# Gated multi-query attention with a SiLU layer: other planner constants, weight pieces split in one go, and O's upper half cast by a transfer

## The chip, the cores and the metric

The kernel runs on one core of one Trainium2 chip. The metric is the device time of one execution in microseconds, the median of several runs. Beside the timed runs there is one profiled execution of the kernel before; "the page" is the summary of its trace, and the other views named below are answers drawn from the same trace.

## The reference

For 2048 rows x of width 512 the kernel computes two branches and mixes them row by row with a gate:

```python
q = (x @ wq).reshape(B, S, 32, 16).transpose(0, 2, 1, 3)     # 32 heads of 16
k, v = x @ wk, x @ wv                                         # one key and value head for all
p = softmax(einsum("bhqd,bkd->bhqk", q, k) * 16 ** -0.5)
a = einsum("bhqk,bkd->bhqd", p, v).transpose(0, 2, 1, 3).reshape(B, S, 512) @ wo
b = silu(x @ w1) @ w2                                         # 512 -> 1792 -> 512
g = sigmoid((x * gate_w).sum(-1, keepdims=True))
out = g * a + (1 - g) * b
```

All in float32: x is (1, 2048, 512), w1 (512, 1792), w2 (1792, 512). The kernel keeps float32 accuracy on a 16-bit matrix engine by writing each operand as an upper and a lower float16 part and adding three products (upper by upper, upper by lower, lower by upper).

## The kernel before, in words

**Tiling.** The rows are in four chunks c of 512, the 32 heads in four groups o of eight. A *round* is one (c, o); there are 16. In a round the 2048 keys are walked in 32 *steps* of 64 keys. A step has two halves j, each with one 128x1024 tile of scores: `scores` (L1224, eight matmuls of 50x32 weights into the PSUM tile `S`, of which there are two), then `exponential` (L1230, ACT, from `S` into half of a probability buffer `P`). So there are 1024 score tiles and 1024 exponentials. There are four buffers `P`, and as the chunks of the input `xs` are used up for good, each of the first three becomes another (`XUSE = "PPP "`).

**P times V.** A finished step is multiplied with V in one of two ways. *Whole* (W): eight float32 matmuls with `VF`, in one go or as two halves N and M of 256 columns each. *Split* (A and B): VectorE (DVE) first computes the lower part of the two halves with two subtractions (`low`, L1236, 128x1024 each, into a tile `L`, a spent weight buffer `raw`, or, in the change, a spent chunk of `xs`); then TensorE takes eight matmuls of the upper bfloat16 half of `P` (A) and eight of the lower part (B). A buffer `P` is free again when W or M has run, or when A and both subtractions have.

**The rest.** The feed-forward layer, the q projections and the output projection are matmuls into `pm` (L848), 64 rows of two different products at a time; a group of eight such matmuls is called a pass F here. An output of the first layer goes through a tanh on ACT (L909), a multiply on DVE (L912), a cast of the upper part by a transfer that GpSimd's queue issues (L921) and a subtraction for the lower (L925).

**What sets the order.** The program is written out once, at build time, by a small planner inside `attention`. It keeps a clock for TensorE (PE), ScalarE (ACT) and DVE with fixed costs (`PASS`, `EXP`, `LOW`, ...) and lets the engine that is free first take its next job; the result is a fixed instruction order for each engine, and on the chip only semaphores wait. For PE the choice is in `pe_next`: scores first (priority 0), then P V that is urgent (1), the feed-forward passes while they are behind their quota (2), other P V (3 or 4), and feed-forward beyond the quota (5). P V is urgent in `pv_next` when

```python
p = 1 if n_exp[0] - 2 * s >= 2 * n_bufs[0] + LAG - 8 or ... else 3 if ab else 4
```

that is, when the exponentials have run so many halves ahead of step s that its buffer is about to be needed. A job that can't be interrupted is taken only if it ends before the next score tile is due, with `SLACK` to spare. DVE's jobs are entries `task(due, ready, length, f)`.

**Weights.** `Pieces` (L159 and on) brings w1, wq, w2 and wo in 36 pieces through two buffers `raw`; `step` (L200) writes the upper part of a new piece (L207) and the lower part of the piece before (L208), and asks GpSimd's queue for the next piece (L190). `piece_next` (L1387) spaces the steps by `PACE`.

**Shifts and the fallback test.** Each of the 15 later q blocks gets a bound that is subtracted from its scores (`q_shift`, L433): 8 rows of 512 numbers go to DRAM (`sh`), and DVE takes their minimum (L440) for a test. The minima, and largest values of inputs and weights, are collected by `chores` one by one on DVE; the flag at the end decides whether a slow second pass runs. With these inputs it doesn't.

**End of a round.** `finish` runs four DVE jobs `norm_a`, `norm_x`, `norm_y`, `norm_b` (transposes and the division), and `norm_c` then splits the result into `O`, upper and lower half (L134, L135), for the output projection of the chunk. The last round does this in two halves (`finish_half`).

## Time and profile before

| what | value |
|---|---|
| median of 3 timed runs | 1021.53 us (1020.79 to 1023.5) |
| the profiled execution's own time | 1022.62 us |
| its span, first to last instruction | 1020.8 us |
| busy: PE, ACT, DVE, POOL | 998.8, 987.1, 913.9, 59.4 us |
| granted TensorE clock | 0.999 |

The profiled execution is 1.09 us above the median of the runs, and its span 1.8 us below its own time. Matmuls and activations overlap the next one of their kind in the trace, so a busy share near 100% doesn't say that an engine runs at its rate: what counts is the distance from start to start. A row of the timeline gives the start, the length of a merged stretch, the engine, the line, what is written from what, and how many instructions are merged; in brackets the idle time before it and what ended that.

### The profile page before, as it was taken

To read this page: it belongs to the slowest core of one execution; us is meant where nothing else is said; L and a number is where in the kernel's file an instruction comes from. 1 tells how busy PE (TensorE), PEld (TensorE's weight loads), DVE (VectorE), ACT (ScalarE), POOL (GpSimd) and SP (SyncE) were. 2 spreads that over 40 slices of the span, in tenths; PEclk is the share of its full clock that TensorE was granted. 3 is DMA by queue.
4 is the path that set the end of the run, shared out by engine and by line. 5 is a ranking of instruction groups with operands and counts; after the bars stand their busy time and mean duration, and the time that the engine had idled before them with its cause. 6 is when DMAs were issued, how large, how long until landed. Compare 5 with 4: busy or idle time off the path is not lost.

```text
span 1020.8 us, 67262 instructions
## 1 busy us (share of the span) xinstructions
PE 998.8 (98%) x31528; PEld 590.4 (58%) x31528; DVE 913.9 (90%) x1177; ACT 987.1 (97%) x1108; POOL 59.4 (6%) x138
## 2 busy tenths in 40 slices
PE   8999999999999999999999999999999999999996
PEld 6455555555555556556565655656565555656754
DVE  7888888889999999999999899999988989889983
ACT  5999999999999999999999999999999999999994
POOL 4111111100000000000000000000000000000000
PEclk9999999999999999999999999999999999999999
DMA  5132321211101111101101111001201110011001
GB/s 210 50 96 77 82 55 53 69 40 41 25 10 45 30 36 20 29 11 35 31 4 42 40 41 25 26 14 26 50 11 25 36 46 15 19 21 25 4 4 47
DMA packets 28105, 39.98 MB, mean 39 GB/s; under 512 B 5689, under 2 KB 19370, under 8 KB 27818
## 3 DMA queue, kind: packets, MB, share of 16 engines
q0 software_dynamic: 10656, 15.73, 7.4%
q1 hardware_dynamic: 16442, 19.27, 5.9%
q8 instruction: 248, 4.06, 1.6%
q10 hardware_dynamic: 720, 0.59, 0.2%
q14 instruction: 39, 0.32, 0.1%
HBM read 19.98 MB, written 8.25 MB: 28 GB/s over the span
## 4 chain that ended last, share of the span: by engine, by line
PE 48%; issue 24%; ACT 17%; DVE 6%; DMA 3%; POOL 1%; SPq 0%; ACTq 0%; POOLq 0%; DVEq 0%
PE pm L848 19%; PE pv L1261 15%; ACT P L1230 12%; PE S L1224 12%; ACT xs L1230 4%; DVE L L1236 2%; DMA raw<-in_B_w_dram 1%; ACT e L909 1%; DVE raw L1236 1%; DMA H<-e 1%; POOL raw L190 1%; DVE e L912 1%; PE pv L1249 1%; DMA xn<-in_A_x_dram 1%; POOL H L921 0%
## 5 line engine op out<-in xcount | busy, mean ns | idle before, releaser
L1230 ACT ACTIVATE P<-S 128x1024 f32<-128x1024 f32 x776 | 741.2, 1094 | 9.3 <-PE pv L1261 3.7
L1224 PE MATMUL S<-qb,KT 50*32 50x512 f16 x8096 | 447.2, 379 | 7.5 <-ACT P L1230 3.5
L1224 PEld LDWEIGHTS <-KT 50*32 50x32 f16 x8096 | 203.2, 89 | 226.3 <-issue 134.0
L1236 DVE TENSOR_TENSOR L<-P 128x1024 f16<-128x1024 f32 x248 | 296.6, 1219 | 28.9 <-ACT P L1230 25.2
L848 PE MATMUL pm<-xs,w1s 64*32 64x512 f16 x5376 | 258.0, 375 | 0.9 <-DVE e L912 0.9
L1230 ACT ACTIVATE xs<-S 128x1024 f32<-128x1024 f32 x248 | 246.7, 1097 | 0.7 <-PE S L1224 0.3
L848 PE MATMUL pm<-w2s,H 64*32 64x512 f16 x5376 | 240.0, 375 | 0.8 <-DVE e L912 0.3
L1261 PE MATMUL pv<-P,VF 64*32 64x512 f32 (+1 forms) x3888 | 225.4, 510 | 0.1
L1236 DVE TENSOR_TENSOR raw<-P 128x1024 f16<-128x1024 f32 x126 | 151.4, 1219 | 6.4 <-ACT P L1230 6.1
L848 PEld LDWEIGHTS <-w1s 64*32 64x32 f16 x5376 | 116.8, 93 | 45.3 <-issue 6.0
L848 PEld LDWEIGHTS <-H 64*32 64x32 f16 x5376 | 112.7, 93 | 43.4 <-issue 4.8
L848 PE MATMUL pm<-xs,wqs 64*32 64x512 f16 x1440 | 101.3, 375 | 0.2
L1236 DVE TENSOR_TENSOR L<-xs 128x1024 f16<-128x1024 f32 x78 | 93.5, 1218 | 4.9 <-ACT xs L1230 4.6
L1261 PEld LDWEIGHTS <-VP 64*32 64x32 f16 x4000 | 75.2, 93 | 34.8 <-issue 4.3
L1261 PEld LDWEIGHTS pv<-P,VF 64*32 64x32 f32 x3888 | 79.6, 106 | 20.6 <-issue 2.4
L1261 PE MATMUL pv<-L,VP 64*32 64x512 f16 x1304 | 88.4, 375 | 0.1
L1261 PE MATMUL pv<-P,VP 64*32 64x512 bf16 x1496 | 83.3, 387 | 0.0
L921 POOL DMA_DIRECT2D H<-e x56 | 29.7, 530 | 709.2 <-DVE e L912 661.9
L848 PE MATMUL pm<-wo_s,O 64*32 64x512 f16 x1440 | 66.3, 375 | 0.1
L1261 PE MATMUL pv<-xs,VF 64*32 64x512 f32 (+1 forms) x1072 | 64.4, 531 | 0.0
L1236 DVE TENSOR_TENSOR raw<-xs 128x1024 f16<-128x1024 f32 x48 | 57.9, 1217 | 4.7 <-ACT P L1230 2.1
L1261 PE MATMUL pv<-raw,VP 64*32 64x512 f16 x696 | 55.2, 375 | 0.0
(215 smaller groups left out, 668.0 us busy)
## 6 DMA issues: line engine op xcount, KB each, us to landing
H<-e POOLq DMA_DIRECT2D x56, 128.0 KB, 2.5
raw<-in_B_w_dram POOLq DMA_DIRECT2D x24, 256.0 KB, 3.2
qb<-qd SPq DMA_DIRECT2D x180, 32.0 KB
xn<-in_A_x_dram SPq DMA_DIRECT2D x8, 512.0 KB
out_dram<-acc SPq DMA_DIRECT2D x14, 256.0 KB
qd<-qx SPq DMA_DIRECT2D x13, 256.0 KB
raw<-in_A_wo_dram POOLq DMA_DIRECT2D x4, 256.0 KB, 3.2
qb<-sh SPq DMA_DIRECT2D x60, 2.0 KB
```

Source lines behind the costliest of these rows:

```text
L190: queue.dma_start(r, src)
L848: nc.tensor.matmul(self.bank[32 * m:32 * m + 32], l(i, rows, 32 * m), r(j, rows), start=first, stop=last)
L909: nc.scalar.activation(e, o.bank, AF.Tanh, scale=t_scale)
L912: nc.vector.scalar_tensor_tensor(e, e, 1.0, o.bank, op0=OP.add, op1=OP.mult)
L921: nc.gpsimd.dma_start(H[:, 0], e)
L1224: nc.tensor.matmul(sc[32 * m:32 * m + 32, f], KT[b:b + 50, k0:k0 + 32], qtile[i][b:b + 50, m // 2, j], start=True, stop=True)
L1230: nc.scalar.activation(probs[s][:, 2 * j:2 * j + 2], banks.pop(p), AF.Exp, scale=scale_of(*rounds[steps[s][0]]))
L1236: nc.vector.tensor_tensor(lows[s, j], probs[s][:, js], upper(probs[s])[:, js], op=OP.subtract)
L1249: nc.tensor.matmul(pvs[i][h][32 * j:32 * j + 32, 256 * q:256 * q + 256], VF[r, NK - 2 * PAIRS + 2 * u + a], probs[s][r, j, 256 * a:256 * a ...
L1261: nc.tensor.matmul(pvs[i][h][32 * j:32 * j + 32, q], a[r], b[r, q], start=k == 0 and n != "B", stop=k == NK - 1 and n in "BMW")
```

## The change

It edits constants of the planner and four pieces of code:

1. `SLACK` 0.1 to 0.05, `LAG` 7 to 6, `GAP` 0.3 to 0.2, and the term `BOW`, which let the feed-forward fall behind its quota by up to 40 passes in mid-program, goes. A step's P V so becomes urgent one exponential sooner.
2. `XUSE`: the third chunk of `xs` becomes four tiles for lower parts instead of a seventh buffer `P`.
3. `Pieces.step` writes both parts of a piece one behind the other, and `piece_next` gives steps later due times.
4. `norm_c` asks GpSimd's queue for a casting transfer for O's upper half; a new DVE job `norm_d` subtracts, planned 3.0 us later.
5. The 15 minima on DVE go; instead 15 transfers on SyncE's queue (`shift_rows`) bring the first halves of the shifts back from DRAM into `wqs` when the last q block is done, and one reduction finds the least.

```diff
-LOAD, SLACK, ROOM, LAG, QUOTA, HB, EB, LB, PACE, START, WAIT, HOLD = 3.5, 0.1, 3.6, 7, 1.7, 7, 2, 3, 5.6, 0.3, 0.2, 0.4
+LOAD, SLACK, ROOM, LAG, QUOTA, HB, EB, LB, PACE, START, WAIT, HOLD = 3.5, 0.05, 3.6, 6, 1.7, 7, 2, 3, 5.6, 0.3, 0.2, 0.4
-BOW = 40 / 2.0 ** 18
-HALVES, GAP = True, 0.3
+HALVES, GAP = True, 0.2
-XUSE = "PPP "
+XUSE = "PPL "
...
         def step(self, by_scalar=False):
-            new = self.raws.pop(0) if self.raws else None
-            if new:
-                r, a1, a2, scale, what = new
-                if by_scalar:
-                    nc.scalar.activation(a1, r, AF.Copy, scale=scale)
-                else:
-                    nc.vector.tensor_scalar(a1, r, scale, None, op0=OP.mult)
-                self.rest.append((what, lambda: nc.vector.scalar_tensor_tensor(a2, r, scale, a1, op0=OP.mult, op1=OP.subtract)))
-            if len(self.rest) > bool(new):
+            while self.rest and (len(self.rest) > 1 or not by_scalar):
                 what, second = self.rest.pop(0)
                 second()
                 self.done.append(what)
                 self.load(nc.gpsimd)
+            if self.raws:
+                r, a1, a2, scale, what = self.raws.pop(0)
+                second = lambda: nc.vector.scalar_tensor_tensor(a2, r, scale, a1, op0=OP.mult, op1=OP.subtract)
+                if by_scalar:
+                    nc.scalar.activation(a1, r, AF.Copy, scale=scale)
+                    self.rest.append((what, second))
+                else:
+                    nc.vector.tensor_scalar(a1, r, scale, None, op0=OP.mult)
+                    second()
+                    self.done.append(what)
+                    self.load(nc.gpsimd)
...
-        return lambda: nc.vector.tensor_reduce(um[:, n:n + 1], s1, axis=AX.X, op=OP.min)
...
+        def shift_rows():
+            for n in range(1, NO * NCH):
+                nc.sync.dma_start(wqs[8 * n - 8:8 * n, 0, 0], sh[n % NO, n // NO][:, 0])
...
-            nc.vector.tensor_reduce(mr[0:64], um, axis=AX.X, op=OP.min)
+            nc.vector.tensor_reduce(mr[0:rows_], wqs[0:rows_, 0, 0], axis=AX.X, op=OP.min)
+            nc.vector.tensor_tensor(mr[0:64], mr[0:64], um, op=OP.min)
...
+                elif XUSE[c] == "L":
+                    l_free.extend((t, flat_x[:, 1024 * n:1024 * n + 1024].rearrange("p (a n) -> p a n", a=2)) for n in range(4))
...
             O = wp.tile([128, 2, 512], F16, name="O", bufs=NO)
-            split_v(O[:, 0], O[:, 1], st["OT"])
+            nc.gpsimd.dma_start(O[:, 0], st["OT"])
+            task(t + CAST + 4, t + CAST, 0.62, lambda t: norm_d(st, key, O, t))
+
+        def norm_d(st, key, O, t):
+            nc.vector.tensor_tensor(O[:, 1], st["OT"], O[:, 0], op=OP.subtract)
...
-                task((n - 4.6) * PACE, max((n - 6) * PACE, t + LOAD if n > 1 else 0.0), 1.3, run)
+                task((n + 1) * PACE, max((n - 1) * PACE, loaded[-2] if len(loaded) > 1 else 0.0), 1.2, run)
...
-                    cands.append((r, 4.5 if near else 2 if work.passes < QUOTA * p + 3 * KD * len(early) - 30 - BOW * p * (2 * len(steps) - p) else 5, "F", None))
+                    cands.append((r, 4.5 if near else 2 if work.passes < QUOTA * p + 3 * KD * len(early) - 30 else 5, "F", None))
```

Because the planner decides anew from the first edit on, the whole order of PE differs. Counted over the first pass, 261 of the 512 steps are split instead of 250, 79 are whole in two halves instead of 54, and 166 whole in one go instead of 202; six steps at the end have a form of their own in both.

**A buffer near the start.** The rows are PE's and ACT's, with buffer numbers. Exponentials are counted from 0; number 34, whose input is `S_1476` before and `S_1497` in the change, writes into `P_576`, which an earlier step still holds. PE before, around the P V of that earlier step:

```order
L1224 LDWEIGHTS KT_60
L1224 MATMUL S_1509<-qb0_83,KT_60 32x512
L1261 MATMUL pv0_791<-P_576,VF_63 32x512
L1261 MATMUL pv1_792<-P_576,VF_63 32x512
L848 LDWEIGHTS wqs_73
```

and the same P V in the change (here the second half of columns, M; N stands one score tile earlier):

```order
L1233 LDWEIGHTS KT_60
L1233 MATMUL S_1385<-qb0_83,KT_60 32x512
L1270 MATMUL pv0_792<-P_576,VF_63 32x256
L1270 MATMUL pv1_793<-P_576,VF_63 32x256
L851 LDWEIGHTS wqs_73
```

ACT before, and then in the change, where these score tiles are used:

```order
L1230 ACTIVATE P_578<-S_1369 128x1024
L1230 ACTIVATE P_575<-S_1392 128x1024
L1230 ACTIVATE P_575<-S_1434 128x1024
L1230 ACTIVATE P_576<-S_1476 128x1024
L1230 ACTIVATE P_576<-S_1509 128x1024
```

```order
L1239 ACTIVATE P_578<-S_1385 128x1024
L1239 ACTIVATE P_575<-S_1424 128x1024
L1239 ACTIVATE P_575<-S_1458 128x1024
L1239 ACTIVATE P_576<-S_1497 128x1024
L1239 ACTIVATE P_576<-S_1537 128x1024
```

Before, the P V that empties `P_576` stands behind both score tiles that are to go into it; in the change it stands ahead of the two tiles before those.

**The end.** DVE's rows from the last transpose of the first half of the last round on. Before:

```order
L1174 STREAM_TRANSPOSE O<-U 128x256
L1150 STREAM_TRANSPOSE T_33427<-pv_31790 128x256
L1150 STREAM_TRANSPOSE T_33427<-pv_31791 128x256
L1154 TENSOR_TENSOR T_33427<-T_33427 128x16x15
L1157 TENSOR_TENSOR U<-T_33427,nus 128x112
```

In the change:

```order
L1179 STREAM_TRANSPOSE O<-U 128x256
L830 SCALAR_TENSOR_TENSOR acc<-pm,gg,acc 128x512
L1155 STREAM_TRANSPOSE T_33593<-pv_31955 128x256
L1155 STREAM_TRANSPOSE T_33593<-pv_31956 128x256
L830 SCALAR_TENSOR_TENSOR acc<-pm,gg,acc 128x512
L1159 TENSOR_TENSOR T_33593<-T_33593 128x16x15
L1162 TENSOR_TENSOR U<-T_33593,nus 128x112
```

Two sums of the output projection (`acc<-pm,gg,acc`) have moved into the last normalisation; on PE the last 4.5 passes of that projection now stand behind the last P V, where before no such pass was left.

More of the change, by code (lines that the diff above doesn't have):

```diff
@@ L109 @@
     kab = consts.tile([128, 32], F16)
-    um = consts.tile([64, NO * NCH], F32)
+    um = consts.tile([64, 1], F32)
     qx = consts.tile([128, 1024], F16)
@@ L131, in split @@
         nc.vector.scalar_tensor_tensor(a2, a, scale, a1, op0=OP.mult, op1=OP.subtract)
-    def split_v(a1, a2, a):
-        nc.vector.tensor_copy(a1, a)
-        nc.vector.tensor_tensor(a2, a, a1, op=OP.subtract)
     def product3(p, lhs, rhs, first, last):
@@ L438, in q_shift @@
             nc.sync.dma_start(sh[o, c][4 * h:4 * h + 4, 0], s1[32 * h:32 * h + 4])
-        n = c * NO + o
-        return lambda: nc.vector.tensor_reduce(um[:, n:n + 1], s1, axis=AX.X, op=OP.min)
     def first_pass(pO):
@@ L722, in chores @@
         todo.append(lambda: absmax(mxs[:, M_VV:M_VV + 1], VF[:, :, 1:17], AX.XY))
+        rows_ = 8 * (NO * NCH - 1)
+        def shift_rows():
+            for n in range(1, NO * NCH):
+                nc.sync.dma_start(wqs[8 * n - 8:8 * n, 0, 0], sh[n % NO, n // NO][:, 0])
         def gather():
             mt, mr, mq = sc[:, 0:32], sc[:, 32:33], sc[:, 64:96]
-            nc.vector.tensor_reduce(mr[0:64], um, axis=AX.X, op=OP.min)
-            nc.vector.tensor_scalar(mxs[0:64, M_B:M_B + 1], mr[0:64], -1.0, SHIFT * LAM / ONE, op0=OP.mult, op1=OP.add)
+            nc.vector.tensor_reduce(mr[0:rows_], wqs[0:rows_, 0, 0], axis=AX.X, op=OP.min)
+            nc.vector.tensor_tensor(mr[0:64], mr[0:64], um, op=OP.min)
+            nc.vector.tensor_scalar(mxs[0:rows_, M_B:M_B + 1], mr[0:rows_], -1.0, SHIFT * LAM / ONE, op0=OP.mult, op1=OP.add)
             nc.vector.transpose(mt, mxs)
@@ L753, in verdict @@
             nc.vector.tensor_copy(flag, g[:, 0, 0:1])
-        return todo, gather, row, *(lambda n=n: check(n) for n in range(0, len(RANGES), 3)), verdict
+        return todo, shift_rows, gather, row, *(lambda n=n: check(n) for n in range(0, len(RANGES), 3)), verdict
     def row_maxima(g0, gs, gp, wqs, qsc):
@@ L884, in x_used @@
                     n_bufs[0] += 1
+                elif XUSE[c] == "L":
+                    l_free.extend((t, flat_x[:, 1024 * n:1024 * n + 1024].rearrange("p (a n) -> p a n", a=2)) for n in range(4))
+                    l_free.sort(key=lambda x: x[0])
                 elif XUSE[c] == "H":
@@ L1037, in shift @@
                 new.wait = t
-                note = q_shift(o, c, s1)
+                q_shift(o, c, s1)
                 shifted.add((o, c))
                 def close(t):
-                    note()
                     open_q.pop()
@@ L1047, in close @@
                         e_left[0] += 1
-                task(t + 9, t, 0.6, close)
+                task(t + 4, t + 2, 0.02, close)
             task(t, t, 0.6, shift, True)
@@ L1385, in pack_next @@
                 task(t + 4, t, length, run)
+        loaded = []
         def piece_next(t):
@@ L1391, in run @@
                     split_pieces.step()
+                    loaded.append(t + LOAD)
                     piece_next(t)
                 n = split_pieces.count
-                task((n - 4.6) * PACE, max((n - 6) * PACE, t + LOAD if n > 1 else 0.0), 1.3, run)
+                task((n + 1) * PACE, max((n - 1) * PACE, loaded[-2] if len(loaded) > 1 else 0.0), 1.2, run)
             else:
@@ L1405, in chore_next @@
             elif len(chores) > 1:
-                task(t + 16, lambda: None if open_q else t, 1.1, lambda t: (chores.pop(1)(), chore_next(t)))
+                task(t + 16, lambda: None if open_q else t + 4, 1.1, lambda t: (chores.pop(1)(), chore_next(t)))
         def finish(i, t):
@@ L1426, in fourth @@
                 norm_b(state)
-                task(t + 6, lambda: t if projected[0] >= NO * c else None, 1.15, lambda t: norm_c(state, (c, o), t))
+                task(t + 6, lambda: t if projected[0] >= NO * c else None, 0.02, lambda t: norm_c(state, (c, o), t))
             task(t, lambda: t if idle[0] else None, 1.25, first)
```

## Prediction

> **What bounds the kernel now.** I read the page first, then the order of start times on ACT, then the list of waits.
>
> ```profile
> span 1020.8 us, 67262 instructions
> PE 998.8 (98%) x31528; PEld 590.4 (58%) x31528; DVE 913.9 (90%) x1177; ACT 987.1 (97%) x1108; POOL 59.4 (6%) x138
> ```
>
> PE and ACT both look full. Starts tell them apart (timeline: start, length, engine, line, what, count):
>
> ```profile
> 25.44 1.94 ACT L1230 ACTIVATE P<-S 128x1024 f32<-128x1024 f32 x2 [0.50 <-PE S L1224]
> ...
> 102.88 0.61 ACT L909 ACTIVATE e<-pm 128x512 f32<-128x512 f32 x1
> 103.35 1.06 ACT L1230 ACTIVATE P<-S 128x1024 f32<-128x1024 f32 x1
> ...
> 478.42 4.74 ACT L1230 ACTIVATE P<-S 128x1024 f32<-128x1024 f32 x5
> 482.94 2.05 ACT L1230 ACTIVATE xs<-S 128x1024 f32<-128x1024 f32 x2
> ...
> 1005.42 2.11 ACT L1230 ACTIVATE xs<-S 128x1024 f32<-128x1024 f32 x2
> ```
>
> From 478.42 to 482.94 five exponentials start, 0.905 us apart; a tanh takes 0.47 to the next start. The program has 1024 exponentials (776 + 248 in the rows below) and 56 tanhs: 1024 x 0.905 + 56 x 0.47 = 953.0 us. From the first start at 25.44 to the last end at 1007.53 ACT takes 982 us for 953 us of work. **ACT has lost 29 us in all**, hidden in part, since an exponential lasts 1.094 and the next may start after 0.905: the first 0.19 us of a bubble is not seen as idle.
>
> PE is next. Its rows, where scores, a whole P V, a feed-forward pass and a split P V follow each other without a wait:
>
> ```profile
> 59.24 0.41 PE L1224 MATMUL S<-qb,KT 50*32 50x512 f16 x8
> 59.46 1.05 PE L1261 MATMUL pv<-P,VF 64*32 64x512 f32 x16
> 60.32 0.41 PE L848 MATMUL pm<-xs,wqs 64*32 64x512 f16 x8
> ...
> 303.66 0.42 PE L1261 MATMUL pv<-P,VP 64*32 64x512 bf16 x8
> 303.89 0.41 PE L1224 MATMUL S<-qb,KT 50*32 50x512 f16 x8
> 304.11 0.39 PE L1261 MATMUL pv<-L,VP 64*32 64x512 f16 x4
> ...
> 304.33 0.42 PE L1261 MATMUL pv<-P,VP 64*32 64x512 bf16 x8
> ...
> 1001.35 0.63 PE L1261 MATMUL pv<-P,VF 64*32 64x256 f32 x16
> 1001.78 1.13 PE L1249 MATMUL pv<-xs,VF 64*32 64x256 f32 x32
> ```
>
> By starts: scores 0.22, a whole P V 0.86, a split one 0.23 + 0.22 = 0.45, a half one 0.43; a pass F 0.215 (it is a 512-column pass as B is). By the order before, PE has 1024 scores, 1704 passes F, 250 split and 262 whole steps: 225 + 366 + 113 + 225 = 929 us of work in the same 982. So ACT is the nearer bound, with 29 us to win at most; PE has 53 us and matters where it makes ACT wait. The waits say how:
>
> ```profile
> DVE L L1236 <- ACT P L1230: 25.2, 40, 2.6
> ...
> ACT P L1230 <- PE pv L1261: 3.7, 5, 1.5
> ACT P L1230 <- PE S L1224: 3.7, 11, 0.5
> PE S L1224 <- ACT P L1230: 3.5, 10, 0.5
> ```
>
> Five times an exponential waited not for its scores but for a P V (a buffer that was not free). With the hidden 0.19 each these five cost 3.7 + 0.95 = **4.6 us**. What is left, 29 - 4.6 = 24 us, is spread over a thousand starts: scores that come a tenth late behind a P V that can't be interrupted.
>
> **The change part by part.**
>
> *P V sooner, new order of PE: buffers.* I went through both orders and took, for each exponential that opens a buffer, the PE work that stands between its own scores and the end of the P V that frees the buffer. Before, five have such work: 1.72 us for number 34 (three passes F, the next score tile and the whole P V that starts at 59.46 above) and 0.86 for numbers 74, 136, 150 and 266, 5.2 us together; the trace charges 4.6 for the same five, so about 0.1 each is absorbed. The worst:
>
> ```profile
> 55.32 3.81 ACT L1230 ACTIVATE P<-S 128x1024 f32<-128x1024 f32 x4
> 60.62 1.94 ACT L1230 ACTIVATE P<-S 128x1024 f32<-128x1024 f32 x2 [1.50 <-PE pv L1261]
> ```
>
> In the change two are left, with 0.75 and 0.43 us: some 0.9 us by the same rate. **-3.7 us** (bounds -4.6, -2.5). That the third chunk no longer gives a seventh buffer shows up here: no such place stands in the last quarter of the order.
>
> *SLACK, GAP, more split steps: late scores.* Eleven more steps are split, which takes 11 x (0.86 - 0.45) = 4.5 us of work from PE; 25 more whole ones in two halves cost 2 x 0.43 = 0.86 as before. PE is not the bound, so this is not time won one for one; it makes scores less late. In the order before, 54 score tiles have more than 0.905 us of other PE work directly ahead of them, 23 more than 1.1; in the change 42 and 14. And a P V may now overrun the next score by 0.05 less. Fewer by a quarter, but of the small latenesses that make up most of the 24 us only some go: I take an eighth, **-3.0 us**. Bounds: +1 (the halves put more changes of job between scores) and -8 (a third).
>
> *DVE: lower parts, casts, minima.*
>
> ```profile
> L1230 ACT ACTIVATE P<-S 128x1024 f32<-128x1024 f32 x776 | 741.2, 1094 | 9.3 <-PE pv L1261 3.7 <-PE S L1224 3.7 <-ACT P L1230 0.3
> ...
> L1236 DVE TENSOR_TENSOR L<-P 128x1024 f16<-128x1024 f32 x248 | 296.6, 1219 | 28.9 <-ACT P L1230 25.2 <-PE pv L1261 1.5 <-ACT xs L1230 0.9
> ...
> L1230 ACT ACTIVATE xs<-S 128x1024 f32<-128x1024 f32 x248 | 246.7, 1097 | 0.7 <-PE S L1224 0.3
> ...
> L1261 PE MATMUL pv<-L,VP 64*32 64x512 f16 x1304 | 88.4, 375 | 0.1
> ...
> L135 DVE TENSOR_TENSOR O<-T,O 128x512 f16<-128x512 f32 x15 | 10.4, 693 | 0.5
> ...
> L440 DVE TENSOR_REDUCE um<-e 64x1 f32<-64x512 f16 x13 | 8.7, 672 | 0.0
> ...
> L134 DVE CAST O<-T 128x512 f16<-128x512 f32 x15 | 6.3, 421 | 0.0
> ```
>
> Added: 22 subtractions x 1.219 = 26.8 us. Removed: 15 casts, 6.3, and 15 minima x 0.67 = 10.1 (one reduction of that size comes back, 0.7). DVE's work grows by 11 to about 925 us of 1016. So far PE has hardly waited for a lower part (0.1 us in the row of pv<-L). In the middle DVE is fuller than its mean (windows of 40 us; the third busy figure is DVE):
>
> ```profile
> 280.00:320.00 40.00, 39.81 (x1267) 22.42 (x1259) 38.63 (x44) 39.17 (x43) 0.00 (x0) 1.00 0.08 23
> 920.00:960.00 40.00, 39.88 (x1365) 27.32 (x1355) 39.04 (x42) 39.94 (x46) 1.58 (x3) 1.00 0.08 15
> ```
>
> There is room for about 1 us in such a window, so some subtractions come late, and B behind them: **+1.0 us** (bounds 0 and +11, all of the added work on the path).
>
> *O's upper half by a transfer.* The same kind of transfer exists, H from e, 56 times:
>
> ```profile
> L921 POOL DMA_DIRECT2D H<-e x56: 528/528/537, 79.8 to 936.6; - x56
> ...
> DMA to landing us min/median/max: 2.2/2.5/4.3
> ```
>
> Fifteen more issues of 0.53 us on a queue that is busy 6%, each behind at most one H issue. The subtraction is planned 3.0 us later, 0.5 more than the median landing. Until then O's lower half is late by 3.5 us, and the projection that reads O waits for no one until its chunk's last round: cover enough, **0**. If a landing takes the 4.3, DVE, in order, stands 1.3 us at the subtraction, and the lower parts queued behind it are late by as much: at most 15 x 1.3 = 19 us of DVE, which has 91 idle but not in the middle.
> The Trainium skill's page "SBUF — State Buffer", section "SBUF: two separate sides", speaks against this edit: descriptors of a transfer issued on GpSimd are written by GpSimd, which is locked out while a DVE operation in a two-port mode runs, a float32 copy within SBUF above all. In this trace all 56 issues took 528 to 537 ns although DVE was busy nine tenths of the time, so the rule doesn't show here. By it long landings would be common, and the sum would move up by as much of the 19 us as falls on the path, into the third rival; by the row it moves by nothing.
>
> *Pieces, shifts.* A piece costs the same two DVE operations either way, and each lands in a `raw` buffer well ahead. The 15 read-backs of 8 KB and the late reduction stand on SyncE's queue and DVE behind the last q block, with no reader but the flag: **0** (bound +1 if a q load queues behind them).
>
> *The end.* Rows of the tail:
>
> ```profile
> 1007.86 1.13 PE L1249 MATMUL pv<-xs,VF 64*32 64x256 f32 x32
> ...
> 1009.06 0.78 DVE L1150 STREAM_TRANSPOSE T<-pv 128x256 f32<-128x256 f32 x2 [1.10 <-PE pv L1249]
> 1009.88 0.41 DVE L1154 TENSOR_TENSOR T<-T 128x240 f32<-128x240 f32 x1
> ...
> 1012.02 1.96 PE L1718 MATMUL pv<-qx,O 128*128 128x512 f32 x4 [1.12 <-DVE O L1174]
> ```
>
> and the sum that has moved in:
>
> ```profile
> L827 DVE SCALAR_TENSOR_TENSOR acc<-pm,gg,acc 128x512 f32<-128x512 f32 x16 | 12.0, 748 | 3.7 <-PE pm L848 3.4
> ```
>
> Now 4.5 passes F (0.97 us) follow the last P V, whose own passes take 0.86: they end at 1007.86 + 0.86 + 0.97 = 1009.7, and with the 0.3 us that now lie between the P V's end (1008.72) and DVE's start (1009.06) the sum can start at 1010.0, ends at 1010.75, and the chain that began at 1009.88 begins there: **+0.9 us** (bounds 0.7 and 1.7).
>
> **Sum:** -3.7 - 3.0 + 1.0 + 0.9 = -4.8 us: the span goes from 1020.8 to 1016.0, the profiled execution's own 1022.6 to 1017.8, and the median of the runs, 1.1 lower, from 1021.5 to **1016.7**.
>
> **Rivals.**
> *Only the planned waits go.* The small latenesses come from rates that differ from the planner's, and return in another order: -3.7 + 0.9 = -2.8 with nothing for late scores and nothing for DVE: 1018.7. For it: 10 waits of PE on ACT stand beside 11 of ACT on PE, so neither is late for long. Against it: fewer late tiles in the order, which no rate changes.
> *PE's work counts in full.* If PE set the pace, 4.5 us less work would be 4.5 us: -3.7 - 4.5 + 0.9 = -7.3: 1014.2. For it: every wait of ACT is one on PE. Against it: PE's 53 us of room.
> *DVE takes over, slower.* In the middle DVE is at 38.6 to 39.0 of 40 us. If the added 11 us land there (or the stalls at O's transfer do), a subtraction is late, B stalls PE in order, and scores behind it; from about 1 us more per window on it decides. Then +11 - 3.7 + 0.9 = +8.2: 1029.7; at half of it +2.7: 1024.2. Against it: the 25.2 us in which DVE waited for exponentials are room too, and the 0.1 us of pv<-L.
> *The change doesn't do what it says*: with PE late, urgency one exponential sooner may put other buffers behind; the count of two places against five speaks against it.
>
> **How the numbers follow.** My forecast 0.40; PE's work in full 0.18; only the planned waits 0.30 (the fourth is in it); DVE slower 0.12. About 0.3% (3.06 us, so 1018.5 and 1024.6) is what a measurement of this kernel can tell. Faster: 0.38 of the forecast's 0.40, 0.18, and 0.03 of the planned waits = 0.59. Slower: 0.09 of DVE's 0.12. Same: the rest, 0.32. The range leaves out the slow half of DVE's case and little on the fast side: 1013 to 1022.
>
> **What would show it.** Right: ACT's waits for P V at two or fewer, below 1 us in all; last exponential's end 5 to 7 us earlier than 1007.5; from there to the end of the span about 14.2 us instead of 13.3; DVE near 925. Wrong: waits of PE on L or of DVE on O's transfer of over a microsecond in sum (DVE's case), or an unchanged end of the last exponential with fewer buffer waits (latenesses returned).

## The result and the profile after

The changed kernel takes 1027.09 us against 1022.14 us of the kernel before (medians of 13 runs each), a ratio of **1.0039** with an interval of 1.0028 to 1.005, taken over all runs (the two medians alone would give 1.0048). It is slower, by 0.4%; 1016.7 us had been predicted. The granted TensorE clock is not the reason: the five of its runs that were granted 0.999 took 1023.4 to 1027.3 us, all above 1022.14. On a second chip the ratio was 1.0021 (1.0011 to 1.0031). The profiled execution's own time is 1027.09 us. Its page, span and busy times:

```profile
span 1025.2 us, 68150 instructions
...
PE 998.6 (97%) x31928; PEld 586.8 (57%) x31928; DVE 926.1 (90%) x1170; ACT 989.8 (97%) x1108; POOL 67.9 (7%) x153
```

ACT's rows of the timeline (start, length, engine, line, what, count, idle time before):

```profile
25.53 1.94 ACT L1239 ACTIVATE P<-S 128x1024 f32<-128x1024 f32 x2 [0.50 <-PE S L1233]
...
52.77 12.05 ACT L1239 ACTIVATE P<-S 128x1024 f32<-128x1024 f32 x13
...
351.20 1.94 ACT L1239 ACTIVATE xs<-S 128x1024 f32<-128x1024 f32 x2 [0.58 <-PE pv L1270]
...
1009.25 1.02 ACT L1239 ACTIVATE P<-S 128x1024 f32<-128x1024 f32 x1 [0.34 <-PE S L1226]
```

Around 60 us, where ACT stood 1.50 us before, thirteen exponentials now run in one stretch; one wait for a buffer of some size is left, at 351. But the last exponential ends at 1010.27 instead of 1007.54, and from there the program needs 14.94 us instead of 13.30. The waits:

```profile
DVE acc L830 <- PE pm L851: 15.2, 19, 2.6
DVE L L1245 <- ACT P L1239: 14.0, 24, 2.4
PE S L1233 <- ACT P L1239: 8.4, 22, 1.0
...
ACT P L1239 <- PE S L1233: 3.9, 10, 0.8
...
PE S L1233 <- issue: 2.0, 4, 0.7
...
PE pm L851 <- issue: 0.8, 3, 0.3
PE S L1226 <- issue: 0.8, 1, 0.8
...
ACT xs L1239 <- PE pv L1270: 0.6, 1, 0.6
...
PE pv L1270 <- DVE L L1245: 0.2, 1, 0.2
```

The row of exponentials that wait for a P V (3.7 us, 5 times, before) has shrunk to 0.6 us. Lower parts are not late: 0.2 us of PE on them, and DVE still waits 14.0 us for exponentials. New are 3.6 us in which PE waited for nothing that the profile shows ("issue", the three rows). Before there was one such row:

```profile
PE S L1217 <- issue: 0.4, 1, 0.4
```

PE's waits for an exponential that still reads the tile for the next scores have grown too, from 3.5 us (10 times) to 8.4 (22 times).

The ledger in the prediction's own measure, the bubbles of ACT (by how much an exponential starts later than 0.905 us after the one before it, or 0.485 after a tanh, summed), gives for one execution of each kernel (the kernel before was not profiled on the second chip):

| | before | changed | changed, second chip |
|---|---|---|---|
| first exponential starts | 25.44 | 25.53 | 25.84 |
| bubbles, exponential waits for a buffer | 5.5 | 2.6 | 2.6 |
| bubbles, scores late | 21.9 | 27.4 | 23.2 |
| last exponential's end to the end | 13.30 | 14.94 | 14.88 |
| span | 1020.84 | 1025.21 | 1021.08 |

The first row of bubbles counts every exponential whose last wait was for a buffer, so it stands above the 4.6 us of the prediction's five places; it fell by 2.9. The second was to fall by 3 us and rose by 1.3 to 5.5; the end was to grow by 0.9 and grew by 1.6.

### The profile page after: what moved, and what is told of

It is laid out like the page before. It is cut to its first block, busy times and chain, and to the rows that moved or that the text cites. A ratio compares the mean times of both kernels' runs of the same rounds, so it can differ in the third digit from the quotient of the medians.

```text
span 1025.2 us, 68150 instructions
## 1 busy us (share of the span) xinstructions
PE 998.6 (97%) x31928; PEld 586.8 (57%) x31928; DVE 926.1 (90%) x1170; ACT 989.8 (97%) x1108; POOL 67.9 (7%) x153
## 4 chain that ended last, share of the span: by engine, by line
PE 56%; ACT 2%; DVE 1%; issue 1%; DMA 0%; ACTq 0%; DVEq 0%
PE pm L851 23%; PE pv L1270 18%; PE S L1233 14%; ACT P L1239 1%; ACT xs L1239 1%; PE pv L1258 1%; DVE L L1245 0%; DMA H<-e 0%; PE S L1226 0%; DVE raw L1245 0%; PE pv L1730 0%; DVE acc L830 0%; DVE H L931 0%; ACT e L915 0%; DVE e L918 0%
## 5 line engine op out<-in xcount | busy, mean ns | idle before, releaser
L1239 ACT ACTIVATE P<-S 128x1024 f32<-128x1024 f32 x802 | 765.2, 1093 | 7.1 <-PE S L1233 3.9
L1233 PE MATMUL S<-qb,KT 50*32 50x512 f16 x8096 | 454.8, 380 | 12.3 <-ACT P L1239 8.4
L851 PE MATMUL pm<-w2s,H 64*32 64x512 f16 x5376 | 247.0, 375 | 1.5 <-issue 0.6
L1239 ACT ACTIVATE xs<-S 128x1024 f32<-128x1024 f32 x222 | 221.7, 1092 | 2.8 <-PE S L1233 1.0
L1270 PE MATMUL pv<-P,VF 64*32 64x256 f32 (+1 forms) x4096 | 223.2, 484 | 0.1
L1245 DVE TENSOR_TENSOR raw<-P 128x1024 f16<-128x1024 f32 x117 | 140.2, 1216 | 6.9 <-ACT P L1239 6.0
L1270 PE MATMUL pv<-P,VP 64*32 64x512 bf16 x1632 | 93.0, 387 | 0.0
L1245 DVE TENSOR_TENSOR L<-xs 128x1024 f16<-128x1024 f32 x58 | 69.2, 1217 | 2.7 <-ACT xs L1239 2.7
L1245 DVE TENSOR_TENSOR xs<-P 128x1024 f16<-128x1024 f32 x45 | 53.3, 1219 | 2.5 <-ACT P L1239 2.4
L918 DVE SCALAR_TENSOR_TENSOR e<-e,pm 128x512 f32<-128x512 f32 x56 | 38.3, 685 | 13.3 <-ACT e L915 12.7
```

The source lines that it names most:

```text
L851: nc.tensor.matmul(self.bank[32 * m:32 * m + 32], l(i, rows, 32 * m), r(j, rows), start=first, stop=last)
L918: nc.vector.scalar_tensor_tensor(e, e, 1.0, o.bank, op0=OP.add, op1=OP.mult)
L1233: nc.tensor.matmul(sc[32 * m:32 * m + 32, f], KT[b:b + 50, k0:k0 + 32], qtile[i][b:b + 50, m // 2, j], start=True, stop=True)
L1239: nc.scalar.activation(probs[s][:, 2 * j:2 * j + 2], banks.pop(p), AF.Exp, scale=scale_of(*rounds[steps[s][0]]))
L1245: nc.vector.tensor_tensor(lows[s, j], probs[s][:, js], upper(probs[s])[:, js], op=OP.subtract)
L1270: nc.tensor.matmul(pvs[i][h][32 * j:32 * j + 32, q], a[r], b[r, q], start=k == 0 and n != "B", stop=k == NK - 1 and n in "BMW")
```

## The experiments

Each comparison is with the kernel before on the same chip; e1 to e4, e5 to e8, e9 to e12 and e13 to e16 ran together on four chips, e17 on a fifth. In the counts of halves in the expectations a step written as two halves counts as two, and the last round's twelve are in them; the table further down counts steps.

**e1, e2: once more, and O's upper half without the transfer.** e1 is the changed kernel unedited. e2 computes the upper half on DVE at the same place of the order:

```diff
-            nc.gpsimd.dma_start(O[:, 0], st["OT"])
+            nc.vector.tensor_copy(O[:, 0], st["OT"])
```

> The changed kernel, not edited, beside the kernel before on one chip. The trace of the changed kernel shows 15 stops of TensorE inside a run of like matmuls, 9.6 us together, at places where no instruction waits for a semaphore; the trace of before shows 8, 4.5 us. If these stops belong to the changed program, this second trace shows 8 us or more of them again, at the same instructions; if they are chance from execution to execution, the sum and the places differ, and the time spreads over several us. Ratio to before expected 1.003 to 1.005.

> The changed kernel with O's upper half cast by VectorE again, at the moment in the order where the transfer was issued; nothing else in the order moves. Transfer theory (the 15 casting transfers disturb TensorE's supply or VectorE's waits): 3 to 5 us faster than the changed kernel, stops inside runs back near 4.5 us. Order theory (the new constants made a worse order): within 1 us of the changed kernel, or slower by up to 2 us since VectorE has 15 x 0.42 us more to do.

Measured: e1 1.0021 (1.0011 to 1.0031), e2 1.0022 (1.0012 to 1.0032). e1 lies a little below what was expected. Its text takes all stops inside runs of like matmuls for stops without a wait, and that is not what the traces say: ten of these stops stand in e1's trace again, at the same instructions and equally long, and in both traces the releaser is an exponential that still reads the tile (8.4 us in 22 waits, and 7.9 in 21). These belong to the order. The stops without a wait are the "issue" rows, 3.6 us in the first trace and 2.4 in e1's.

The transfer is neither cost nor gain. Its rows in the changed kernel, from the groups and from the transfers (KB, median us to landing):

```profile
L1185 POOL DMA_DIRECT2D O<-T x15 | 8.0, 535 | 304.4 <-PE S L1233 186.0 <-DVE T L1179 118.4
```

```profile
H<-e POOLq DMA_DIRECT2D x56, 128.0 KB, 2.4
...
O<-T POOLq DMA_DIRECT2D x15, 128.0 KB, 3.0
```

The fifteen issues took 531 to 557 ns (535 is their mean), and DVE never waited for one of the transfers, though they landed after 3.0 us (median) and not the 2.5 that the prediction took over from H. By the rule of the Trainium skill's page "SBUF — State Buffer" (section "SBUF: two separate sides") that the prediction weighed, an issue that meets a float32 copy of DVE within SBUF is held up. During its issue none of the fifteen met one: fourteen ran beside a subtraction for a lower part, one beside a scaling that reads `pm`. So these runs neither show the rule nor speak against it.

**e3, e4: the constants apart from the rest.** e3 is the changed kernel with the old SLACK, LAG, GAP and BOW; e4 is the kernel before with the new ones.

```diff
-LOAD, SLACK, ROOM, LAG, QUOTA, HB, EB, LB, PACE, START, WAIT, HOLD = 3.5, 0.05, 3.6, 6, 1.7, 7, 2, 3, 5.6, 0.3, 0.2, 0.4
+LOAD, SLACK, ROOM, LAG, QUOTA, HB, EB, LB, PACE, START, WAIT, HOLD = 3.5, 0.1, 3.6, 7, 1.7, 7, 2, 3, 5.6, 0.3, 0.2, 0.4
-HALVES, GAP = True, 0.2
+HALVES, GAP = True, 0.3
+BOW = 40 / 2.0 ** 18
...
```

> The changed kernel with SLACK, LAG, GAP and BOW as before; the other four edits stay. Order theory: back to the time of before or 1 to 3 us below it, since the tail has no feed-forward pass left behind the last P V (the order shows none) and the end from the last exponential on is 13.3 us again. Transfer theory: still 3 us or more above before, less 1.6 us for the tail.

> The kernel before with the new SLACK, LAG, GAP and no BOW; the other four edits left out. Order theory: 3 to 5 us slower than before, as the changed kernel is; the order has 5 places with a buffer freed behind its scores (as before) and 12 matmuls of the output projection behind the last P V. Transfer theory: within 1.5 us of before.

Measured: e3 **0.9986** (0.9977 to 0.9995), e4 **1.0077** (1.0064 to 1.009). The four pieces of code bring a little; the constants cost all of the loss and more. In the kernel before they cost more than the 3 to 5 us expected, 7.1, and much of that at the end: e4 needs 17.54 us from the last exponential on, 4.2 more than the kernel before.

**e5 to e8: each constant alone in the kernel before.** e5 has LAG 6, e6 SLACK 0.05, e7 GAP 0.2. (BOW was not taken out alone. It is out in e4 and in all versions from e9 on, e12 among them, which is faster than the kernel before.) e8 has HOLD 0.41 instead of 0.4, a new plan with the same counts.

```diff
-LOAD, SLACK, ROOM, LAG, QUOTA, HB, EB, LB, PACE, START, WAIT, HOLD = 3.5, 0.1, 3.6, 7, 1.7, 7, 2, 3, 5.6, 0.3, 0.2, 0.4
+LOAD, SLACK, ROOM, LAG, QUOTA, HB, EB, LB, PACE, START, WAIT, HOLD = 3.5, 0.1, 3.6, 6, 1.7, 7, 2, 3, 5.6, 0.3, 0.2, 0.4
```

```diff
-LOAD, SLACK, ROOM, LAG, QUOTA, HB, EB, LB, PACE, START, WAIT, HOLD = 3.5, 0.1, 3.6, 7, 1.7, 7, 2, 3, 5.6, 0.3, 0.2, 0.4
+LOAD, SLACK, ROOM, LAG, QUOTA, HB, EB, LB, PACE, START, WAIT, HOLD = 3.5, 0.05, 3.6, 7, 1.7, 7, 2, 3, 5.6, 0.3, 0.2, 0.4
```

```diff
-HALVES, GAP = True, 0.3
+HALVES, GAP = True, 0.2
```

```diff
-LOAD, SLACK, ROOM, LAG, QUOTA, HB, EB, LB, PACE, START, WAIT, HOLD = 3.5, 0.1, 3.6, 7, 1.7, 7, 2, 3, 5.6, 0.3, 0.2, 0.4
+LOAD, SLACK, ROOM, LAG, QUOTA, HB, EB, LB, PACE, START, WAIT, HOLD = 3.5, 0.1, 3.6, 7, 1.7, 7, 2, 3, 5.6, 0.3, 0.2, 0.41
```

> The kernel before with LAG 6 in place of 7 and nothing else: a P V is urgent one exponential sooner. Theory (late scores: an urgent P V taken sooner stands ahead of score tiles and ends too late for them): LAG is the largest part of the constants' +7 us, so 1.003 to 1.006 of the kernel before, although the order has fewer places where a buffer is opened late (4 with 3.4 us of TensorE work instead of 5 with 5.2). Rival (end: the constants cost by what they leave behind the last P V): in this order 44 matmuls of the output projection stand behind the last exponential's P V, the most of all versions, so the span after the last exponential grows by 2 to 3 us and the rest is unchanged: 1.002 to 1.003. Rival (any new plan costs a little, since the constants were chosen by timing): like e8_replan, within 0.002 of it.

> The kernel before with SLACK 0.05 in place of 0.1 and nothing else. By the counts of the order (8 places with a late buffer, 12.5 us of TensorE work, instead of 5 with 5.2; 58 late score tiles instead of 54) the theory of late buffers gives +6 us, 1.006. Rival (end: no matmul of the output projection is left behind the last P V here): 1.000 within 0.001.

> The kernel before with GAP 0.2 in place of 0.3 and nothing else. By the counts of the order (4 places with a late buffer, 5.8 us instead of 5.2; 55 late score tiles instead of 54; nothing left behind the last P V) every theory but chance says 1.000 within 0.0015.

> The kernel before with HOLD 0.41 in place of 0.40, a change of a hundredth of a microsecond in one of the planner's due times, which orders TensorE a little differently and leaves every count as it was (250 split steps, 5 late buffers with 5.2 us). It measures what a plan that is as good by the counts costs or brings by chance. Theory (late scores, buffers and the end decide): 1.000 within 0.001. Rival (two plans differ by whatever stops they happen to meet): up to 0.004 to either side, with the difference in the stops inside runs of like matmuls where nothing waits for a semaphore (4.5 us before, 9.6 in the changed kernel).

Measured: e5 1.0023 (1.0012 to 1.0034), e6 **1.0227** (1.0214 to 1.024), e7 **1.0124** (1.0106 to 1.0141), e8 0.9999 (0.999 to 1.0008). A new plan as such is no loss. e5's end is 15.06 us, 1.8 longer, as the rival of the end had it; but that rival left the rest unchanged, and in the profiled execution, the slowest of e5's nine, the last exponential also ends 3.9 us later. So LAG 6 alone in the kernel before is a small loss. e6 and e7 missed every expectation, because each meets large waits of its own. e6, ACT's timeline:

```profile
53.63 5.62 ACT L1230 ACTIVATE P<-S 128x1024 f32<-128x1024 f32 x6
73.67 0.60 ACT L909 ACTIVATE e<-pm 128x512 f32<-128x512 f32 x1 [14.42 <-PE pm L848]
74.16 6.59 ACT L1230 ACTIVATE P<-S 128x1024 f32<-128x1024 f32 x7
```

ACT, in order, waits 14.42 us for the input of a tanh, and exponential 34 behind it needs a P V that ends later still. On PE both stand behind feed-forward passes, and among these PE itself waits 5.4 us for DVE in four stops. The count of the order had such places, but not what PE waits for in them. e7 has a second kind, among its waits:

```profile
ACT xs L1230 <- PE S L1224: 5.3, 6, 2.8
...
DVE sc L743 <- DMA ident<-md: 4.1, 1, 4.1
```

DVE, in order, waited 4.1 us for a row of the fallback test to come back from DRAM, the lower parts behind it were late, then B, then a score. e6 has the same wait, with 6.0 us. So the constants can't be added up one by one: alone they open holes that they don't open together. Together, in e4 and in the changed kernel, no such hole is left, and the loss is of another kind.

**e9 to e12: which constant it is in the changed kernel.** e9 sets SLACK back to 0.1, e10 SLACK and LAG (only GAP 0.2 is left), e12 SLACK and GAP (only LAG 6 is left). e11 keeps all and puts the last projection ahead of P V once all scores are planned.

```diff
-LOAD, SLACK, ROOM, LAG, QUOTA, HB, EB, LB, PACE, START, WAIT, HOLD = 3.5, 0.05, 3.6, 6, 1.7, 7, 2, 3, 5.6, 0.3, 0.2, 0.4
+LOAD, SLACK, ROOM, LAG, QUOTA, HB, EB, LB, PACE, START, WAIT, HOLD = 3.5, 0.1, 3.6, 6, 1.7, 7, 2, 3, 5.6, 0.3, 0.2, 0.4
```

```diff
-LOAD, SLACK, ROOM, LAG, QUOTA, HB, EB, LB, PACE, START, WAIT, HOLD = 3.5, 0.05, 3.6, 6, 1.7, 7, 2, 3, 5.6, 0.3, 0.2, 0.4
+LOAD, SLACK, ROOM, LAG, QUOTA, HB, EB, LB, PACE, START, WAIT, HOLD = 3.5, 0.1, 3.6, 7, 1.7, 7, 2, 3, 5.6, 0.3, 0.2, 0.4
```

```diff
-                    cands.append((r, 4.5 if near else 2 if work.passes < QUOTA * p + 3 * KD * len(early) - 30 else 5, "F", None))
+                    cands.append((r, 0.5 if p >= 2 * len(steps) - 0 else 4.5 if near else 2 if work.passes < QUOTA * p + 3 * KD * len(early) - 30 else 5, "F", None))
```

```diff
-LOAD, SLACK, ROOM, LAG, QUOTA, HB, EB, LB, PACE, START, WAIT, HOLD = 3.5, 0.05, 3.6, 6, 1.7, 7, 2, 3, 5.6, 0.3, 0.2, 0.4
+LOAD, SLACK, ROOM, LAG, QUOTA, HB, EB, LB, PACE, START, WAIT, HOLD = 3.5, 0.1, 3.6, 6, 1.7, 7, 2, 3, 5.6, 0.3, 0.2, 0.4
-HALVES, GAP = True, 0.2
+HALVES, GAP = True, 0.3
```

> The changed kernel with SLACK back at 0.1 and the rest as it is (LAG 6, GAP 0.2). In this order no buffer is opened late, no matmul of the output projection stands behind the last P V (36 in the changed kernel), but 51 score tiles are late instead of 42. Theory of the end (what stands behind the last P V is half of what the constants cost, 2.0 us of 3.9): the span after the last exponential falls from 14.9 to 12.9 us and the time to 0.999 to 1.000 of the kernel before (the changed kernel: 1.002 to 1.004). Rival (LAG 6 itself: P V that is urgent sooner makes scores late): stays at 1.002 or above.

> The changed kernel with LAG 7 and SLACK 0.1 back, so that of the new constants only GAP 0.2 is left. The order has nothing behind the last P V, 2 late buffers with 1.3 us, and as few late score tiles (42) as the changed kernel. Theory of the end, and the rival of LAG 6 alike: 0.998 to 0.999, the same as with all old constants. If GAP is what costs (halves of a P V begun although other work comes ready soon): 1.001 or above.

> The changed kernel with one more rule: from the moment the last score tile has been issued in the plan, the feed-forward's queue (now the output projection) goes ahead of P V. It moves the passes ahead of the last ten score tiles and leaves five whole P V behind the last one; nothing of the projection stands behind the last P V; all before is as in the changed kernel. Theory of position (it is the sum behind the last P V that delays the last normalisation): the span after the last exponential falls from 14.9 to 13.0 to 13.5 us, 0.9985 of the changed kernel. Rival (backlog: TensorE has 4.6 us of work left after the last score tile, whichever kind it is, and five P V are 4.4): 14.5 us or more, no change against the changed kernel, 1.002 to 1.004 of the one before.

> The changed kernel with SLACK 0.1 and GAP 0.3 back, so that of the new constants only LAG 6 is left. The order has no late buffer, nothing behind the last P V, 48 late score tiles. Theory of the end: 0.998 to 0.999, the best of all, since the buffers are won and nothing is lost at the end. Rival (LAG 6 itself): 1.001 or above, as the kernel before with LAG 6 alone (1.0023).

Measured: e9 1.0076 (1.0052 to 1.01), e10 1.0036 (1.0023 to 1.0049), e11 1.0033 (1.0019 to 1.0048), **e12 0.998** (0.9967 to 0.9992). LAG 6, the change that the words "P V urgent sooner" name, is no loss with the new code, and e12 is the best version so far. e10 falls on the side on which GAP costs. e9's number is the one its rival named, LAG 6 itself, but e12 rules that rival out. The theory of the end is not enough: e10 has a short end (12.4 us) and is slow, and e9's end is 14.5 us although nothing of the projection stands behind its last P V. In e11 the end did not shrink either:

```profile
1009.50 1.02 ACT L1239 ACTIVATE P<-S 128x1024 f32<-128x1024 f32 x1 [0.34 <-PE S L1226]
...
1010.86 1.48 PE L851 MATMUL pm<-wo_s,O 64*32 64x512 f16 x24
...
1012.63 1.23 PE L1258 MATMUL pv<-P,VF 64*32 64x256 f32 x26
...
1013.96 0.78 DVE L1155 STREAM_TRANSPOSE T<-pv 128x256 f32<-128x256 f32 x2 [0.17 <-PE pv L1258]
```

The P V now comes after the projection and ends by as much later; 15.26 us from the last exponential to the end. So it is the backlog of PE behind the last score, whatever its kind, as the rival in e11's text had it. e9 also met a hole, which speaks of edit 5:

```profile
ACT P L1239 <- PE S L1233: 11.1, 21, 4.8
...
DVE sc L729 <- DMA wqs<-sh: 4.8, 1, 4.8
PE pv L1270 <- DVE xs L1245: 4.5, 2, 3.8
```

The one reduction over the shifts waits 4.8 us for the read-back, and PE and ACT stand behind it near 745 us.

**e13 to e16: the number of halves.** Both SLACK 0.05 and GAP 0.2 make the planner write more whole P V as two halves. e13 has the old GAP alone; e14 and e15 have LAG 6, SLACK 0.1 and GAP 0.4 or 0.25; e16 is e12's kernel again.

```diff
-HALVES, GAP = True, 0.2
+HALVES, GAP = True, 0.3
```

```diff
-LOAD, SLACK, ROOM, LAG, QUOTA, HB, EB, LB, PACE, START, WAIT, HOLD = 3.5, 0.05, 3.6, 6, 1.7, 7, 2, 3, 5.6, 0.3, 0.2, 0.4
+LOAD, SLACK, ROOM, LAG, QUOTA, HB, EB, LB, PACE, START, WAIT, HOLD = 3.5, 0.1, 3.6, 6, 1.7, 7, 2, 3, 5.6, 0.3, 0.2, 0.4
-HALVES, GAP = True, 0.2
+HALVES, GAP = True, 0.4
```

```diff
-LOAD, SLACK, ROOM, LAG, QUOTA, HB, EB, LB, PACE, START, WAIT, HOLD = 3.5, 0.05, 3.6, 6, 1.7, 7, 2, 3, 5.6, 0.3, 0.2, 0.4
+LOAD, SLACK, ROOM, LAG, QUOTA, HB, EB, LB, PACE, START, WAIT, HOLD = 3.5, 0.1, 3.6, 6, 1.7, 7, 2, 3, 5.6, 0.3, 0.2, 0.4
-HALVES, GAP = True, 0.2
+HALVES, GAP = True, 0.25
```

> The changed kernel with GAP 0.3 back, SLACK 0.05 and LAG 6 as they are. The order has as many halves as the changed kernel (170, SLACK alone makes them), 3 late buffers, 48 late score tiles, 8 matmuls behind the last P V instead of 36. Theory 1 (the number of halves costs): 1.001 to 1.004 of the kernel before, less 0.001 at most for the shorter end. Theory 2 (GAP's rule costs, whatever their number): 0.998 to 0.9995.

> The changed kernel with SLACK 0.1, LAG 6 and GAP 0.4: fewer halves than in any version (70), one late buffer with 1.7 us, 36 matmuls of the projection behind the last P V as in the changed kernel. Theory 1: the late scores fall below those of LAG 6 alone, by about 1 us; with 1.7 us for the buffer and 2 us at the end 0.999 to 1.001. If fewer halves cost too (a whole P V that can't be interrupted makes scores later than two halves do): above 1.002, with the bubbles behind whole P V grown.

> The changed kernel with SLACK 0.1, LAG 6 and GAP 0.25: 138 halves, no late buffer, nothing behind the last P V. Theory 1, and theory 2 as well: between LAG 6 alone (0.998) and LAG 6 with GAP 0.2 (1.0076, of which a stall of TensorE on a subtraction near 745 us is 6 us): 0.999 to 1.002.

> The kernel of e12 once more (the changed kernel with SLACK 0.1 and GAP 0.3 back, LAG 6), on the chip of this comparison: 0.997 to 0.9992 if its gain is a property of the order, about 1.000 if the first value was chance.

Measured: e13 1.004 (1.0027 to 1.0052), e14 1.0057 (1.0044 to 1.007), e15 1.0009 (0.9999 to 1.0019), e16 **0.9985** (0.9976 to 0.9993). e13 stays slow with the old GAP and e10 was slow with the old SLACK: neither rule is needed for the loss, and the number of halves, high in both, fits. e15 lies between, as expected. e14, with the fewest halves, is slow again, against theory 1. Its trace says where, against e16: 2.3 us more of bubbles at buffers (one of 1.55 at 283.6), an end of 14.81 instead of 12.35, and 1.7 us more of late scores. Of the last, 1.5 us are scores behind a whole P V (9.8 us against 8.3), the sign that e14's text gives for a cost of too few halves.

**e17: halves by themselves.** The order of e12, with 177 whole P V written as two halves behind each other:

```diff
-            pv(s, n)
+            for m in "NM" if n == "W" and s < ends_at and 0 < steps[s][1] < NK - 1 else n:
+                pv(s, m)
```

> The kernel of e12 (LAG 6 alone of the new constants, 0.998 and 0.9985) with 177 of its 195 whole P V written as two halves directly behind each other: the same order, the same sums, 354 halves more. If a half costs by itself (an extra half of about 0.03 to 0.05 us, as the trend from 110 to 200 halves in the other versions would have it, some 5 us for 90 of them): 8 to 15 us more, 1.006 to 1.013. If it costs only by where the planner puts it: 0.9975 to 0.9995, no change.

Measured: **1.0186** (1.0171 to 1.0202), far on the side of a price of its own. Against e12 and e16 (0.998 and 0.9985) that is 2.03% or 20.8 us for 177 steps, **0.117 us for a whole P V written as two halves**; by the spans, 1036.73 against 1017.55 (the mean of e12 and e16), 0.108. The matmuls themselves don't take longer. The same place in e12 and e17, PE's timeline:

```profile
493.69 1.05 PE L1270 MATMUL pv<-P,VF 64*32 64x512 f32 x16
494.55 0.41 PE L1270 MATMUL pv<-L,VP 64*32 64x512 f16 x8
```

```profile
501.05 1.23 PE L1270 MATMUL pv<-P,VF 64*32 64x256 f32 x32
501.92 0.58 PE L1270 MATMUL pv<-L,VP 64*32 64x512 f16 x8
```

0.86 and 0.87 us from start to start, as the prediction had it; over all pairs that run undisturbed the median is 0.864, against 0.860 for whole ones in e12. (The ends of matmuls are modelled.) What grew are stops in which PE waits for nothing. e17's busy times, instruction packets and waits:

```profile
PE 1008.1 (97%) x34296; PEld 640.5 (62%) x34296; DVE 927.6 (89%) x1170; ACT 995.6 (96%) x1108; POOL 67.6 (7%) x153
...
q8 instruction: 270, 4.42, 1.8%
```

```profile
PE pm L851 <- issue: 5.3, 11, 0.9
...
PE pv L1270 <- issue: 1.7, 3, 1.1
...
PE S L1233 <- issue: 1.4, 3, 0.9
```

and of e12:

```profile
PE 996.4 (98%) x31464; PEld 588.4 (58%) x31464; DVE 926.4 (91%) x1170; ACT 988.3 (97%) x1108; POOL 67.5 (7%) x153
...
q8 instruction: 248, 4.06, 1.7%
```

```profile
PE pv L1270 <- issue: 0.4, 1, 0.4
...
PE pm L851 <- issue: 0.4, 1, 0.4
...
PE S L1233 <- issue: 0.3, 1, 0.3
```

The three rows make 8.4 us in 17 stops, against 1.1 in e12. Counted from start to start, where the 0.16 us hidden under the matmuls ahead belongs to a stop too, these 17 cost 11.1 us, and with shorter ones all stops without a wait come to 19.5 us in e17 and 4.9 in e12: 14.6 of the 19.2 us between the spans.

So 0.117 us is an average and not a price that each pair pays. The scores of e12 and e17 stand in the same order, in 1036 groups of eight matmuls, and can be set side by side: e17's last group starts 19.5 us further behind e12's than its first, 17.8 us of that at the 101 intervals that differ by more than 0.1 us, 0.6 at the 825 that differ by no more than 0.025. From e12's 575.7 to 761.4 us, with 33 of the P V written as pairs, e17 did not fall behind at all (185.7 us in e12, 185.6 in e17).

2832 matmuls and as many weight loads more, 5664 instructions, came with 22 more instruction packets of 16 KB, one for about 257. One of the stops, PE's timeline of e17:

```profile
568.89 0.54 PE L1233 MATMUL S<-qb,KT 50*32 50x512 f16 x8
569.11 0.61 PE L851 MATMUL pm<-wo_s,O 64*32 64x512 f16 x11
570.57 0.40 PE L851 MATMUL pm<-wo_s,O 64*32 64x512 f16 x5 [0.85 <-issue]
```

PE stops amid sixteen like matmuls, none of which waits for a semaphore. In e17's transfer records an instruction packet landed at 569.14, 1.43 us before it went on. It is the same at every one of the 17 stops: PE resumed 1.35 to 1.60 us after a packet had landed, though packets come only about every 3.8 us (270 in 1037). Six of the eight in the changed kernel resumed 1.42 to 1.51 us after one (the other two, in the last 20 us, 1.25 and 0.61), e12's three 1.39 to 1.58, and the one of the kernel before 1.38. That these stops are waits for instructions is read from this distance; no run changes the supply.

## Why the prediction was wrong

The versions with the changed kernel's code, one profiled execution each; the counts of steps are from the orders, the excess over e12 and e16 (mean 0.99825) from the measured ratios and 1021 us:

| | steps in halves | bubbles at buffers | late scores | end | excess, us | 0.113 a step + end + buffers |
|---|---|---|---|---|---|---|
| e14 | 29 | 2.9 | 25.7 | 14.81 | 7.6 | 2.5 |
| e3 | 49 | 2.6 | 21.2 | 12.93 | 0.4 | 2.5 |
| e12, e16 | 50 | 0.8, 0.6 | 24.1, 24.0 | 11.98, 12.35 | 0 | 0 |
| e15 | 63 | 1.3 | 23.7 | 13.03 | 2.7 | 2.9 |
| changed (two chips) | 79 | 2.6 | 27.4, 23.2 | 14.94, 14.88 | 5.8, 3.9 | 7.9 |
| e13 | 79 | 1.7 | 27.6 | 13.75 | 5.9 | 5.9 |
| e10 | 94 | 1.8 | 27.7 | 12.36 | 5.5 | 6.3 |

The last column adds 0.113 us (the middle of e17's two values) for each step in halves beyond 50, and what end and buffers of that trace exceed e12's and e16's means by. e17's price is an average over stops, measured at other places of the order than these, so it is an estimate; it follows the excess of e15, e13 and e10 within 1 us, is 2 to 4 us too high for the changed kernel, 2 for e3, and fails for e14. Left out are e9, whose hole covers the rest, and e2 and e11, which have the changed kernel's 79 steps and an excess of 4.0 and 5.2 us.

- *Buffers, -3.7*: right. The five places charged 4.6 us before, the two left charge 1.07: 3.5 us won. (By the prediction's own rate their 1.18 us of work give 1.0 and not 0.9.)
- *Late scores, -3.0 (bounds +1 and -8)*: **wrong, and the step that failed.** They rose by 5.5 us on one chip and 1.3 on another. Two sentences of it fell. "25 more whole ones in two halves cost 2 x 0.43 = 0.86 as before" holds from start to start and not for the program: e17 shows about 0.11 us for each on the average, which would be 2.8 us for the 25. And the count of late tiles in the order (54 to 42) said nothing about time: e10 has 42 of them too and is slow; 48 stand in the order of e12 and e16, which is fast, and 48 in e13's, which is slow. The count assumes that PE keeps its rate.
- *DVE, +1.0*: DVE's work came out at 926.1 us as computed (925), and PE waited 0.2 us for lower parts; 0 would have been right. That rival fell, though the times it named, 1024.2 to 1029.7 us, enclose the 1027.09 measured: that is chance.
- *O's cast by a transfer, 0*: right (e2).
- *Pieces and shifts, 0*: right in this order, in which the reduction did not wait. The reason given was wrong: "no reader but the flag" forgets that DVE is in order. In e9 the same reduction stalls DVE for 4.8 us.
- *The end, +0.9 (0.7 to 1.7)*: mis-sized, but within its bounds; +1.6. The rows:

```profile
1010.25 1.14 PE L1258 MATMUL pv<-P,VF 64*32 64x256 f32 x32
...
1011.55 2.12 PE L851 MATMUL pm<-wo_s,O 64*32 64x512 f16 x36 [0.16 <-issue]
...
1013.73 0.75 DVE L830 SCALAR_TENSOR_TENSOR acc<-pm,gg,acc 128x512 f32<-128x512 f32 x1 [1.50 <-PE pm L851]
1014.39 0.40 DVE L1159 TENSOR_TENSOR T<-T 128x240 f32<-128x240 f32 x1
```

  I had divided 36 matmuls by eight: 4.5 passes, 0.97 us. They are a lone product, with nothing of another beside it, so they run as nine groups of four at about 0.22 us each: 2.0 us from 1011.55 to the next job at 1013.61. The chain of the last normalisation, which waits for the sum in front of it on DVE, starts at 1014.39, 4.1 us after the last exponential; before, 2.3.
- *Rivals*: "only the planned waits go" came nearest in its mechanism, latenesses that return in another order, but it had them come back in equal size. "PE's work in full" and DVE's case fell. "The change doesn't do what it says" fell too: the buffers were won.
- *What would show it*: waits for P V below 1 us, and DVE near 925, came as said. The last exponential's end was to come 5 to 7 us earlier and came 2.7 later; the text had read an unchanged end with fewer buffer waits as latenesses that return, and that is what the traces show.

What is shown: the constants are the cause, in the changed kernel SLACK and GAP and not LAG (e3, e10, e12, e13, e16; in the kernel before LAG 6 alone costs 2 us, e5), and whole P V written as two halves cost time although each pair takes as long as one (e17). What stays open: how much of the loss of one order is its halves, how much its end, and how much chance. Stops in "issue" explain 3.6 us of the changed kernel's trace and 1.1 of e12's, so 2.5 us of a loss of 4 to 6; on the second chip they are 2.4.

A rival for the rest was not tested. PE's waits for exponentials that still read the score tile are 8.4, 7.9, 7.5 and 7.2 us in the four executions of the changed order (the changed kernel, e1, e2, e11), 3.0 in e12 and in e16, 2.2 in e3 and 3.5 before; e14 has 6.0 and e13 4.7, but e10, which also lost time, only 3.2. An order in which PE stands more often may lack that time at other scores; no run changes these waits alone. Why few halves don't help in e14 is accounted for in its trace, not explained.

## What to carry to other kernels

An edit that writes the same work as more instructions is not free because the matmuls take the same time from start to start: where TensorE takes some 62 matmuls and weight loads in a microsecond, count them, and look for stops in which nothing is waited for. In this change a count of late places in the planned order predicted the waits it was made for (the five buffers came out within 0.2 us; in e6 it did not), and not a sum of small latenesses; for those, change one constant at a time and time it. And a value that "no one waits for" still blocks an engine that reads it in order.

The best version is e12's: all of the change but with SLACK 0.1 and GAP 0.3 as before, at 0.998 and 0.9985 on two chips.

## What the runs showed of the hardware that I had not expected

- TensorE stops where nothing holds it that the profile shows, and then goes on 1.35 to 1.60 us after a 16 KB instruction packet has landed (17 stops in e17, 8.4 us in all): it looks as if instructions ran short. Only e17, with 68,592 matmuls and weight loads, stands out. Below that the number of instructions alone doesn't tell: with 62,928 the stops make 1.1 and 0.4 us (e12, e16) but 3.7 in e5, with 63,856 from 0.9 (e2) to 3.6 (the changed kernel), with 64,336 1.4 (e10). What limits the supply is not shown.
- The same program varies by some microseconds. Two profiled executions of the changed kernel on two chips differ by 4.1 us of span, all in late scores (27.4 and 23.2 us), and its runs went from 1020.8 to 1030.4 us, those of e12 and e16 from 1017.4 to 1023.1.
- A group of four matmuls of 64 rows takes as long as one of eight when no second product stands beside it: nine groups of four in the last projection start 0.21 to 0.22 us apart, as groups of eight do (0.215).
